# Windowed attention with a mixture of experts: another order for all engines, from a table

## The chip, the cores and the metric

The kernel runs on one core of one Trainium2 chip. The core has five engines with a queue of instructions each: PE (TensorE, matmuls, with its weight loads shown apart as PEld), DVE (VectorE), ACT (ScalarE), POOL (GpSimd) and SP (SyncE, which here only issues transfers). An engine runs its own instructions in the order in which they were written, and waits on semaphores for results of others and, in some cases, for its own. The metric is device time in microseconds (us), the median of several runs.

## What is computed

Two stages, with 8 batches, 8 heads, 576 positions, 64 columns a head. The first is attention with a window of 128 positions and a linear bias by distance; its output x of 576 x 512 a batch goes into the second, a mixture of four experts, of which each position uses its best two. Each expert is a causal attention with one head of 64 columns and an output projection to 512 columns.

```python
mask = (rel >= 0) & (rel < window)
scores = np.where(mask, scores + bias[None], -1000000000.0)
...
for e in range(E):
    q = x @ wq[e]; k = x @ wk[e]; v = x @ wv[e]
    scores = np.where(causal, -1000000000.0, scale * (q @ k.transpose(0, 2, 1)))
    ...
    ye = a @ v @ wo[e]
    for kk in range(K):
        mask = topk[:, :, kk] == e
        out += mask[..., None] * w[:, :, kk:kk + 1] * ye
```

## The kernel before

Work is cut by pairs of heads (four a batch, `g` counts all 32) in the first stage, and by batches `b` and pairs of experts `pr` in the second. A pair of heads is done in these steps: `attn_s` makes the scores of two blocks of 128 queries in one PSUM bank, `wrap` (L459) moves the far half of a window's columns over the near half with a masked copy on DVE (`copy_predicated`, two blocks of 128 columns at once), and `blocks` (L466) runs for each block a DVE instruction that adds the bias, scales and finds the row's minimum `nm` (CUSTOM_DVE_ANT_0 in the profile, ISA in the listings of the order; the read of its minimum, of shape 128x1, is a row of its own), and then an exponential on ACT. `normalise` (L472) sums and inverts on DVE and scales the rows (`scl`). `attn_t` transposes on PE; `split` (L561) writes the result apart on DVE. `attn_pv` (L597) multiplies with V, adds partial sums and writes x as two numbers, a rounded high part and the rest, into a tile named `wx`; the last 64 columns go through a small tile `xq` and then through `tail_out` (L644): a copy that rounds (CAST in the profile), and a subtraction. The second stage has projections with the same split into high and low parts (`QHm`, `KKm`, `AHm`, `ALm`), a gate per position, scores with minima `mnm`, normalising factors `mr` (L818), transposes (L837) and the output projection `moe_wo` (L895). Tiles named `w` are general work buffers of several pools, `ps` are the eight PSUM banks.

None of this is issued as it is written. The calls go to a recorder (`_Rec`), and some have an alternative: `evac` (a copy out of PSUM) and the copies of `tail_out` may go to ACT or DVE, `rnd` and `scl` to POOL or ACT, `ssub` to DVE or POOL. `plan` (L201) unpacks a table of numbers, `ORDER` (from L38 on), in which each number is a step back or forth in the list of recorded operations, times two, plus which of the alternatives to take; a negative place is a filler matmul, issued at the start. `place` (L160) then gives each tile a buffer of its pool in that order: a buffer is free again after the last operation on its old tile. The loop at L1190 issues the result, so nearly every row of the profile has line L1191. The order of each engine's queue, SP's transfers among them, thus follows from the table alone:

```python
    for lo, hi in zip(z[:n], z[n:]):
        d = lo + 256 * hi
        at += (d >> 1) ^ -(d & 1)
        ...
        i = nodes[at // 2]
        out.append(alt.get(i, [ops[i]])[at % 2])
```

Of the kernel before, what the change touches and what calls it, by code (L numbers as in the profile page):

```python
# [19 lines left out]
B, H, S, D = 8, 8, 576, 64  # L20
DM = H * D
E = 4
P = 128
# [27 lines left out]
    "W%a(atbaL<bLmqfAZ&%3z5M7=4nvLgXh1&{r;bFokbswGSIt(bK2%Mape~zLU-ryA%0<$-vCUNp*j4h+W73JD+c((Y=zB_Q26v~5IB&n;AbLe90|Ss&<Fg"
    "_IHVWhSKig$RjL2*#uK6?<*5|YpRqa{$Qmw_%Ff8B<~BIvk4#)i7OVv@Pa-_S9o^GgswC>y;YqPQ+pZ?t6vd?|u}rnAa;_(>)HhbbhR#Z}b7EI$k<;$12M"
    "b2aatJUBFpxl^>GZwr2YV|K_xK<@n8)j5aZ>zC<!#Z26pz&z(gw}LBaO{nl}e#n9j<iK!37<kZP1xt)YPk{5kk~C#a?M+v(Ws1|A7>$$u6d3MJv?P2Z{Zj"
    "Ihc<QPu$+f>17VtX+POrtgLHPp}L{b&g6*9?|g)@-(>H=Op61!>P>Hd>0QU@wCnpvJGs(V&{Wui-8F7s(jbHrqSy)3vVHTo5IjD2p>XVDF>iAgzvp67WEN"
    "FE@b`EzMuYhKB{R}x!YY6KWg6icUjF9S>=SdU;dR$vz0oMKFV5#lpKrDKl({w<pUucvcvo@*G9TrSw07WEtE>?!tF)#lpD-Iw=Z0E-v!XQqgVtgxUF?mfk"
    "tuSr+fGtqAeK2&Zcv^LKmaVqEH)z2$I(2%4vr2_y)GzA<`7_&h;&;&DA~>>UImBm66WZhgiJyzY-F;GM#BE`Jvy(rGu4SZ$LzL3M<$pXrcbjovwLq`g(_R"
    "Al2W3^v&iV(n=ia`9hq)6H6yieXVD$bNawsCcSXLf`>^wA;ZNW9YZAOt^aj7i{kRNQ%b@~FX5l(CZl<b>(A*|JagmfJuK7NF;aU_~pW}~igJlapwhHqQr="
    "m)J@ajyNmAtfkYFU8ge&090@$#S1#3ObLjDs6wLR>$2#|VGZ;RXnYSR{o5%q5K9%=83Zf^OyZAr7d}_ld**^wS%E@ju`8b__I@(<2+OQ$`-haDWjyeBfzl"
    "Qf2hq8N7b{eYK~)8fZUv<iz~MtbJkK#uUdCxwCmZ;b6|GiUB$mPoMf~1W@-ve6zmt)i^{G;>GYoRJgJ32#{?Rl}fRGkpe67NuPO9ls;J(uFzJzgrs(JKt0"
    "mR%Im7vyTD%QCM?RQT+^BgD&p)duI&Ey68GfREj{<~ke9#p(cdEPcSO`3HBM#ExYjn6*I$FGc-VqcC@TRUlw1Nx_Q5(!PdlvbesDj+r6>IdInyaNEL{*zw"  # L60
    "@&s4bCP_K5o6@^e%W#DW^56b2hE|$zAOCcW=J|B%3~jk&Dq-Izo4le8Zct%8PME|<P7U>8m_zXOJ9FS=M!O<8_O;w93nAnjkdsoe1HF>Sp|uGhL9$9jX6^"
    "i8{lXk3_n33?4!eBedU0k!2CVrg?oL2tMyREi9aX0HaEh>{r91l`xh%~PVeQom$a5^Dzx028lSJNQKf%`(Y=@m;!cfq#ipjv|0Ryciq=(~%HJb~6UK$!1G"
# [1216 lines left out]
```

## Time and profile before

| | |
|---|---|
| median of 3 runs | 500.97 us (500.94 to 501.03) |
| the profiled execution | 501.47 us |
| its span in the trace | 499.4 us, so 2.1 us lie around it |
| mean granted clock of PE | 0.998 |
| busy PE, PEld | 482.0 us, 411.5 us |
| busy DVE, ACT, POOL | 428.3 us, 365.1 us, 221.1 us |

A row of the profile names the line, the engine, the operation and its tiles as output<-input. Busy time of PE has modelled ends. An engine's share of the chain that ended last is the time that lay on that one path through all engines, so it is smaller than its busy share. The waits list, for a pair of waiting and awaited engine, the time in total, how often and the longest. Two rows of one engine may overlap in time: the next instruction can start while the one before it is still finishing.

### The profile page before, as it was taken

The numbers are of one execution on the slowest core, as the hardware profiler recorded it, in microseconds if no ns is written. First come the engines' busy times: TensorE is split into PE (matmuls) and PEld (weight loads), VectorE is DVE, ScalarE is ACT, GpSimd is POOL, SyncE is SP. The second block draws the span as 40 slices with busy tenths as digits, with TensorE's granted clock in tenths as the row PEclk, the third lists the DMA queues.
The fourth block names the chain that finished last, engine by engine and source line by source line (L and its number), as shares of the span: only waits on it lengthen the run. The fifth ranks groups of instructions, "written<-read, shape, count | busy, mean of one in ns | idle before, by whom it ended". The sixth has DMA issues, their size and how long they took to land.

```text
span 499.4 us, 17525 instructions
## 1 busy us (share of the span) xinstructions
PE 482.0 (97%) x6380; PEld 411.5 (82%) x6380; DVE 428.3 (86%) x1936; ACT 365.1 (73%) x1375; POOL 221.1 (44%) x456
## 2 busy tenths in 40 slices
PE   7999999999999999999999999999999999999996
PEld 5788888897788788798898987988778798799875
DVE  6999999989997999679988899798998979965842
ACT  5757878978878479596887869688786776853862
POOL 4724957072826205434461525707073523534250
PEclk9999999999999999999999999999999999999999
DMA  8879142107233035060442323620234031200033
GB/s 211 255 189 240 44 122 58 30 22 171 77 118 81 3 95 159 16 164 3 122 132 78 81 62 100 168 59 8 72 125 125 3 79 28 85 3 1 4 106 106
DMA packets 29862, 44.99 MB, mean 90 GB/s; under 512 B 9424, under 2 KB 15824, under 8 KB 29776
## 3 DMA queue, kind: packets, MB, share of 16 engines
q1 hardware_dynamic: 29040, 43.42, 31.8%
q8 instruction: 50, 0.82, 0.7%
q10 hardware_dynamic: 736, 0.46, 0.3%
q14 instruction: 36, 0.29, 0.2%
HBM read 34.42 MB, written 9.44 MB: 88 GB/s over the span
## 4 chain that ended last, share of the span: by engine, by line
PE 45%; DVE 35%; POOL 6%; ACT 5%; issue 4%; DMA 3%; SPq 1%; ACTq 0%; DVEq 0%; POOLq 0%
PE ps L1191 45%; DVE w L1191 21%; DVE ps L1191 6%; POOL w L1191 5%; ACT w L1191 4%; DMA w<-in_hd 2%; DVE mr L1191 1%; SPq L1191 1%; DVE ALm L1191 1%; DMA w<-in_wall 1%; DVE r L1191 1%; DVE wx L1191 1%; DVE KKm L1191 1%; DVE MPL L1191 1%; DVE nm L1191 0%
## 5 line engine op out<-in xcount | busy, mean ns | idle before, releaser
L1191 ACT COPY w<-ps 128x256 f32<-128x256 f32 (+2 forms) x217 | 87.7, 441 | 36.7 <-PE ps L1191 25.8
L1191 PE MATMUL ps<-wx,WH 128*128 128x288 f32 (+2 forms) x512 | 112.1, 303 | 1.8 <-DVE nm L1191 1.5
L1191 ACT ACTIVATE w<-w,nm 128x128 f32<-128x128 f32 x252 | 99.0, 396 | 17.1 <-DVE nm L1191 15.9
L1191 POOL TENSOR_SCALAR w<-w,r 128x128 f32<-128x128 f32 x176 | 66.1, 387 | 100.5 <-DVE mr L1191 29.7
L1191 POOL TENSOR_SCALAR w<-w,mr,w 128x512 f32<-128x512 f32 (+3 forms) x128 | 80.0, 634 | 45.0 <-DVE ps L1191 13.5
L1191 PEld LDWEIGHTS ps<-wx,WH 128*128 128x128 f32 x512 | 83.1, 189 | 5.2 <-DVE nm L1191 3.0
L1191 ACT ACTIVATE w<-w,mnm 128x512 f32<-128x512 f32 (+3 forms) x128 | 71.1, 557 | 17.2 <-DVE mnm L1191 16.5
L1191 DVE CUSTOM_DVE_ANT_0 w<-ps,tbt 128x128 f32<-128x128 f32 x288 | 72.9, 285 | 5.8 <-PE ps L1191 2.8
L1191 DVE TENSOR_TENSOR w<-ps,tmt 128x768 f32<-128x768 f32 (+3 forms) x96 | 72.3, 772 | 1.8 <-PE ps L1191 1.2
L1191 PE MATMUL ps<-wx,WL 128*128 128x288 f32 (+2 forms) x256 | 71.9, 297 | 0.0
L1191 PE MATMUL ps<-idt,w 64*128 64x64 f32 (+1 forms) x1152 | 62.1, 231 | 6.3 <-POOL w L1191 2.3
L1191 PE MATMUL ps<-w 64*64 64x192 f32 (+3 forms) x1256 | 62.9, 305 | 1.4 <-DVE nm L1191 0.7
L1191 PE MATMUL ps<-WH,wx 128*128 128x260 f32 x288 | 63.8, 288 | 0.2
L1191 PEld LDWEIGHTS ps<-idt,w 64*128 64x128 f32 (+1 forms) x1152 | 48.9, 139 | 18.3 <-POOL w L1191 6.0
L1191 PE MATMUL ps<-w,vt 64*64 64x192 f32 (+4 forms) x1344 | 59.2, 284 | 1.3 <-DVE nm L1191 0.7
L1191 PEld LDWEIGHTS ps<-w,vt 64*64 64x64 f32 (+1 forms) x1344 | 49.5, 133 | 8.4 <-issue 1.6
L1191 PEld LDWEIGHTS ps<-w 64*64 64x64 f32 (+1 forms) x1256 | 47.2, 134 | 10.8 <-DVE nm L1191 2.4
L1191 DVE COPY_PREDICATED ps<-mkt,ps 128x256 f32<-128x256 int32 (+2 forms) x160 | 50.6, 330 | 0.9
L1191 DVE CUSTOM_DVE_ANT_0 w<-ps,mtt 128x256 f32<-128x256 f32 (+2 forms) x96 | 50.2, 553 | 1.2 <-PE ps L1191 0.4
L1191 PEld LDWEIGHTS ps<-WH,wx 128*128 128x128 f32 x288 | 48.0, 189 | 2.0 <-DVE nm L1191 0.3
L1191 DVE COPY w<-ps 128x256 f32<-128x256 f32 (+3 forms) x93 | 42.5, 477 | 7.9 <-PE ps L1191 7.6
L1191 PE MATMUL ps<-w,w 128*64 128x64 f32 (+4 forms) x576 | 48.3, 319 | 0.3 <-DVE w L1191 0.2
(110 smaller groups left out, 961.6 us busy)
## 6 DMA issues: line engine op xcount, KB each, us to landing
w<-in_hd SPq DMA_DIRECT2D x56, 288.0 KB, 4.2
vt<-in_vd SPq DMA_DIRECT2D x28, 320.0 KB, 4.0
out<-w SPq DMA_DIRECT2D x31, 256.0 KB, 3.0
w<-in_hd SPq DMA_DIRECT2D x14, 128.0 KB, 3.9
w<-in_hd SPq DMA_DIRECT2D x56, 32.0 KB, 3.4
w<-in_wall SPq DMA_DIRECT2D x4, 386.0 KB, 5.5
out<-w SPq DMA_DIRECT2D x8, 128.0 KB, 2.4
vt<-in_vd SPq DMA_DIRECT2D x4, 192.0 KB, 4.6
```

What stands on the lines that cost most here:

```text
L1191: getattr(getattr(tc.nc, e), m)(*a, **k)
```

## The change

The table `ORDER` is replaced by another one, two lines shorter; nothing else is edited. The line that issues is L1189 instead of L1191. Operations, tiles and transfers are the same, and which buffer and which of its alternative engines an operation gets follows from the new table. The new table was made with a model in which VectorE and GpSimd wait for their own last result.

```diff
 ORDER = (
-    "c-p;re_Ui)b!WYIPrZBT_onO3)N`uVst5|PP?!M&89G7)1%+&pfd~m~U_!az!e_vMf&qnT$bf>vPNQ_}j`Ro$hTcFzo9<co1Pmy>(_~=-3LnA14j33|2NG"
...
+    "c-p;KeOO#sdB69bckVgKy_*?3v(C6PEBMS*Xc<c?bfFFvTIT7{9onHn1q&8jMnfAOVI35@ObZH?C_IHND7cB6)I>p{5*sSG@RU@dpu{B=Y_N$2g{NSHCKf"
...
 )
```

Of the table the diff can show no more than that it is another. What stands in the queues: DVE has 1,935 rows before and 1,902 now, ACT 838 and 880, POOL 459 and 454 instructions, PE 4,792 matmuls in both. DVE's instructions that wait for the result of the instruction straight ahead of them on DVE are 215 before and 109 now. POOL's are 50 and 45.

The first place is on DVE, in the scores of a pair of heads (the trace of before has it at 93.7 to 95.5 us). `ps` are PSUM banks with scores, `w` the tile of the probabilities, `nm` the minima; DVE_49 after "waits" is a wait for DVE's own earlier result, PE_49, Pool_49 and Activation_49 for the other engines. Before:

```order
L1191 COPY_PREDICATED ps_71<-mkt,ps_71 128x2x128 [waits PE_49]
L1191 ISA w_87,nm_183<-ps_71,tbt 128x128 [waits DVE_49]
L1191 ISA nm_183 128x1
L1191 ISA w_87,nm_183<-ps_71,tbt 128x128
L1191 ISA nm_183 128x1
L1191 COPY_PREDICATED ps_69<-mkt,ps_69 128x2x128 [waits PE_49]
L1191 ISA w_87,nm_183<-ps_69,tbt 128x128 [waits DVE_49]
L1191 ISA nm_183 128x1
L1191 ISA w_87,nm_183<-ps_69,tbt 128x128
```

Now:

```order
L1189 COPY_PREDICATED ps_73<-mkt,ps_73 128x2x128 [waits DVE_49,PE_49]
L1189 TENSOR_TENSOR ALm<-ps_74,AHm 128x512 [waits Activation_49]
L1189 ISA w_84,nm_183<-ps_73,tbt 128x128 [waits DVE_49,Pool_49]
L1189 ISA nm_183 128x1
L1189 ISA w_84,nm_183<-ps_73,tbt 128x128
L1189 ISA nm_183 128x1
L1189 COPY_PREDICATED ps_70<-mkt,ps_70 128x2x128 [waits PE_49]
L1189 ISA w_84,nm_183<-ps_70,tbt 128x128 [waits DVE_49]
L1189 ISA nm_183 128x1
L1189 COPY_PREDICATED ps_72<-mkt,ps_71 128x64 [waits PE_49]
L1189 ISA w_84,nm_183<-ps_70,tbt 128x128
```

Before, each pair of minima stands right behind the masked copy that it reads. Now the first masked copy has the subtraction that makes `ALm` behind it, and a third masked copy stands between the two minima of `ps_70`, the first of which still follows its own copy.

The second place is on DVE in `attn_pv` and `tail_out` (111 us in the trace of before): `xq` is the small tile, `wx` the tile of x. Before:

```order
L1191 TENSOR_TENSOR w_101<-w_101,ps_70 128x448 [waits PE_49]
L1191 TENSOR_TENSOR ps_75<-xq_184,ps_70 128x64 [waits Activation_49]
L1191 CAST wx_80<-ps_75 128x64 [waits DVE_49]
L1191 TENSOR_TENSOR wx_80<-ps_75,wx_80 128x2x64 [waits DVE_49]
L1191 COPY xq_198<-ps_71 128x64 [waits PE_49]
L1191 TENSOR_TENSOR ps_71<-xq_198,ps_76 128x64 [waits DVE_49]
L1191 TENSOR_TENSOR w_104<-w_104,ps_76 128x448 [waits Activation_49]
```

Now:

```order
L1189 TENSOR_TENSOR w_101<-w_101,ps_76 128x448 [waits PE_49]
L1189 TENSOR_TENSOR w_92<-ps_74,tmt 128x2x2x64
L1189 TENSOR_TENSOR ps_69<-xq_184,ps_76 128x64 [waits Activation_49]
L1189 TENSOR_TENSOR KKm<-ps_71,KKm 128x288
L1189 TENSOR_TENSOR wx_79<-ps_69,wx_79 128x2x64 [waits Activation_49]
L1189 COPY xq_198<-ps_70 128x64 [waits PE_49]
L1189 TENSOR_TENSOR ps_70<-xq_198,ps_75 128x64 [waits DVE_49]
```

and on ACT, now, at the same work:

```order
L1189 CAST KKm<-ps_71 128x288 [waits PE_49]
L1189 COPY xq_184<-ps_69 128x64 [waits PE_49]
L1189 CAST wx_79<-ps_69 128x64 [waits DVE_49]
L1189 ACTIVATE ex<-ex 128x5x4 [waits Pool_49]
L1189 COPY w_104<-ps_72 128x512 [waits PE_49]
L1189 CAST wx_81<-ps_70 128x64 [waits DVE_49,PE_49]
```

The rounding copy into `wx_80` stood on DVE between two instructions that need one another's results; it is on ACT now (`wx_79`), behind the copy of `xq`, and DVE has the subtraction for `KKm` between the sum and the subtraction that reads it.

## Rows read from the trace of the kernel before

**Rows 1.** The page: span, busy time by engine, chain that ended last.

```profile
span 499.4 us, 17525 instructions
...
PE 482.0 (97%) x6380; PEld 411.5 (82%) x6380; DVE 428.3 (86%) x1936; ACT 365.1 (73%) x1375; POOL 221.1 (44%) x456
...
PE 45%; DVE 35%; POOL 6%; ACT 5%; issue 4%; DMA 3%; SPq 1%; ACTq 0%; DVEq 0%; POOLq 0%
```

**Rows 2.** Busy time in three windows; the first line names the columns.

```profile
core 0: us, PE busy (x) PEld busy (x) DVE busy (x) ACT busy (x) POOL busy (x), PEclk, DMA share, GB/s
50.00:75.00 25.00, 24.71 (x382) 22.24 (x381) 24.64 (x113) 20.31 (x84) 17.73 (x39) 1.00 0.31 82
75.00:100.00 25.00, 24.46 (x335) 21.08 (x328) 23.99 (x126) 22.77 (x92) 10.55 (x21) 1.00 0.18 44
200.00:225.00 25.00, 24.55 (x313) 21.47 (x312) 17.90 (x87) 17.78 (x68) 11.03 (x21) 1.00 0.35 90
```

**Rows 3.** Waits of PE's weight loads: total us, times, longest us.

```profile
PEld ps L1191 <- DVE nm L1191: 8.6, 20, 1.1
...
PEld ps L1191 <- POOL w L1191: 6.2, 16, 0.8
...
PEld ps L1191 <- DVE w L1191: 4.9, 20, 0.4
...
PEld ps L1191 <- ACT w L1191: 4.5, 13, 1.2
...
PEld ps L1191 <- DVE mnm L1191: 3.0, 12, 0.4
```

**Rows 4.** DVE's timeline in the scores: start us, duration us, then the instruction.

```profile
93.78 0.42 DVE L1191 COPY_PREDICATED ps<-mkt,ps 128x256 f32<-128x256 int32 x1
94.24 0.29 DVE L1191 CUSTOM_DVE_ANT_0 w<-ps,tbt 128x128 f32<-128x128 f32 x1
...
94.45 0.29 DVE L1191 CUSTOM_DVE_ANT_0 w<-ps,tbt 128x128 f32<-128x128 f32 x1
...
96.83 0.42 DVE L1191 COPY_PREDICATED ps<-mkt,ps 128x256 f32<-128x256 int32 x1
97.16 0.16 DVE L1191 RECIPROCAL mr<-mr 128x1 f32<-128x1 f32 x1
97.23 0.27 DVE L1191 CUSTOM_DVE_ANT_0 w<-ps,tbt 128x128 f32<-128x128 f32 x1
```

**Rows 5.** DVE's timeline in `tail_out`.

```profile
111.48 0.22 DVE L1191 TENSOR_TENSOR ps<-xq,ps 128x64 f32<-128x64 f32 x1
111.74 0.22 DVE L1191 CAST wx<-ps 128x64 fp32r<-128x64 f32 x1
```

**Rows 6.** Copies out of PSUM by form: busy us, mean ns, then idle before.

```profile
L1191 ACT COPY w<-ps 128x512 f32<-128x512 f32 x95 | 54.0, 588 | 13.5 <-PE ps L1191 12.0 <-ACT AHTm L1191 0.6
...
L1191 ACT COPY w<-ps 128x256 f32<-128x256 f32 x66 | 23.2, 374 | 15.1 <-PE ps L1191 8.9 <-DVE lg L1191 5.6
...
L1191 DVE COPY w<-ps 128x512 f32<-128x512 f32 x31 | 20.9, 683 | 2.5 <-PE ps L1191 2.4
...
L1191 DVE COPY w<-ps 128x256 f32<-128x256 f32 x38 | 15.2, 416 | 4.0 <-PE ps L1191 3.9
...
L1191 ACT CAST wx<-ps 128x64 fp32r<-128x64 f32 x18 | 3.6, 208 | 2.1 <-DVE ps L1191 1.6 <-DVE mr L1191 0.4
...
L1191 DVE CAST wx<-ps 128x64 fp32r<-128x64 f32 x14 | 3.0, 218 | 0.2
```

**Rows 7.** Scalings and subtractions with a choice of engine, by form.

```profile
L1191 POOL TENSOR_SCALAR w<-w,r 128x128 f32<-128x128 f32 x176 | 66.1, 387 | 100.5 <-DVE mr L1191 29.7 <-DVE r L1191 19.7 <-DVE ps L1191 15.1
...
L1191 ACT ACTIVATE w<-w,r 128x128 f32<-128x128 f32 x112 | 39.9, 395 | 7.0 <-DVE r L1191 5.6 <-DVE wx L1191 1.1
...
L1191 POOL TENSOR_TENSOR wx<-w,wx 128x512 fp32r<-128x512 f32 x16 | 20.6, 1290 | 2.4 <-ACT wx L1191 1.7
...
L1191 DVE TENSOR_TENSOR wx<-w,wx 128x512 fp32r<-128x512 f32 x12 | 9.0, 749 | 1.7 <-POOL wx L1191 1.3 <-ACT wx L1191 0.5
```

More of the change, by code (lines that the diff above doesn't have):

```diff
@@ L111 @@
[L111 to L113 removed]
+    "c-p;KeOO#sdB69bckVgKy_*?3v(C6PEBMS*Xc<c?bfFFvTIT7{9onHn1q&8jMnfAOVI35@ObZH?C_IHND7cB6)I>p{5*sSG@RU@dpu{B=Y_N$2g{NSHCKf"
+    "6vY18-Id*=f-Yd`+z<zw#Lk8|GhzQ6bP{@x>q!mqqZIPsVeKYrOmGCYuFQ>%z-v8K{;h(b;Yo><!;<0MQmKgl4wblhq4x~Nh`ed(9xr+Q%|MU6nTiZGR#Z"
@@ new lines @@
+    "7iPxD*~#vIGGwEmPQ9aSsJs_AHUGCP}W}wETDQ)B1~=}&#Lq+yHpktsz@cXQCc6ORm?4aWJCUU#^8l_?ziudJWAZ&%sn)ub$`b*yz8`8vE}BG_JdXMusb-"
+    "_LvrcPz*^=+Q*-n*tX%E31QzE??nQ6G{A6)p0ono+`TqQ}Ebzd4q>QgW$6oi`u@mcWhYz0rG9~OWcR>__Q?}BcE`VH^%wa7NJGh{}*LNcb#r-hQI1SJXD@"
+    "%}@?-z19r}`|)!^OPGw!CwtMR=M;m~9H0ak(c!JI+!UovE;8Qk%nE&~$#}qJ^-D@_XKeIcEO^yc0qmfHeLfEn-&HM;FW!aB&3Y7=Q{z&=o4{^;Sb2^*IYX"
+    "h1AJXoq1V#R<OIki7)M@tD(HCAYo>h@M!b3;N$_Afl2<`F?Myi+*PzQVqx=nFdQllK$hRvGwhnZUo(6;pjecd6JL7ZyleHW`qQW_)#vX9#Y0n$KjVM?qvh"
@@ new lines @@
+    "=ohWOD1XFBlLQu{|A*l7v*=m;a!#uT;zA%K4MDn7EeR8cbSFAliQ6xvevp%9<|^8I)tIL_YwsSo!3=DR+e>8F+9YSxbzRSI60O6}loQQOS7F0-58e(pX0q"
+    "*AJy5g{3`{l<28O?Hbh`?}AcHxM)BBJ6FS>$Y`wo{yw5=LjKor=K=QoB2JGH$DL&5^)6V#ACJCQ=R9QW?a?9S87rr&Ff@smNQOv4P6V0y1r%g%vS(Z!b@)"
+    "-4-buoVe-H#{}HQ!X|<%3%#1fwltLK}dZ!itH9@2#2z9mfZh%xL`j{%zqOj`#a{v!J+v*zBsnEHZxkBB@+9t&^WMNijv8p!OpK^Qd!j+jt!ft=(yEo6lbv"
+    "TXBECd~maBX(9X>53Gtv*n^1);J~ruKTo^6=96hhYmupyp-|X(MdS`|D4+gBQ*YncL5%V^-RGm^(zRRTSuZ|8Ub6of@Cm+s8Mvl<1eg6meA`Lgq_T0hV9_"
@@ new lines @@
+    "Hem~6jW_XxkG`}5=g&-6=fZ{)!Of55ryl$KXIEFVa<lReKxrb)JJ-qT;=<QfM}H64!M@|MFJAe?r!3h4wSc|mgj&j)x`w{$Gj*E5Y&ENdq+1Gsdc4pB{X_"
+    "le+$w<4>tW(v7=);+cH_=gv@KXx)!-<8ph3O%EMbhWE||h^v)2p#BtY1`-ZQmM$I5(5_sXW)<fWd`e&%H5iY<D6<oubuP*&7;al2z~f2VE@SS5SYQ`xo;z"
+    "Quq<^<+hOmOb(K*2OhyFI&ix``L@8<HKqtQ!b7i2z1vBaL;QzJdZI0SyD3+=mz$apFT8BSJi`ivCAu)_-_rqBjFR|KV_TUr4Vvm0|P*#_6UavCPz6`l>Vx"
+    "82FfuX0vPsz4y&rR0CQWcn92++%}OUIk#>Azy0@?#7E+hb^n0vu$-Aie1YRrkstBmOjO<JW>5@=7=dePieDd9-VBWnta<M141H&_E#j8uJv(-Habwu%XT+"
@@ L114 @@
+    "BSf2M#*ESfiJny_Bi%^7@8adaSV2-psM90Q#Ms_~Nc4se5}mFTmsni&>VPz=CI2cCA-SY*AfsR=dj3iAjkiPwiDImhYFkJGHNDzqj-=y@$|M$oN9+L+t%M"
+    "p1HbJ~3w!tMOq!UR#<?71dYoeE6uIE8W?6KfdDPIq0n-^lNO-i(BiOoVjgs4j|DY>mCiI^FYfmq{sNckPvV@Xg*(k`y{LHJrBDNBqJh&Gy}cuAFz@k~OJM"
+    ";@(*jGiOr*2E^sAqG1v0b;d6-w_d$H*C0jL5O$vqR!=Dz&M`aI`PU}p(f3Pc2Lb?llXIFTw<S$9P!vI-;o|sMUz^0;s5jaFN-3z!T"
 )
```

130 lines of the change are left out of this document (56 added, 74 removed).

## The prediction

> **What bounds the kernel now.** I read the page first: the busy shares and the chain that ended last [rows 1]. PE is busy for 482.0 of 499.4 us (97%), DVE for 428.3 (86%), ACT for 365.1 (73%), POOL for 221.1 (44%). By shares alone PE is the bound, and only 499.4 - 482.0 = 17.4 us would be left to win. The chain says more: 45% of it is PE, 35% DVE, 6% POOL, 5% ACT. PE's ends are modelled, so a PE that is called busy may be waiting inside a modelled duration; the chain then passes through DVE.
>
> Second, the busy time by stages [rows 2]. From 50 to 75 us DVE works 24.64 us of 25.00 and from 75 to 100 us 23.99, level with PE (24.71 and 24.46). From 200 to 225 us DVE has 17.90 and PE still 24.55. So there are stages in which DVE feeds PE with nothing in hand, and stages in which its speed can't matter. ACT's worst stretch is 22.77 of 25.00, from 75 to 100 us.
>
> Third, what PE's weight loads wait for [rows 3]: DVE's row minima nm for 8.6 us in 20 waits, DVE's w for 4.9 in 20, DVE's mnm for 3.0 in 12: 16.5 us in 52 waits. POOL's w costs 6.2 and ACT's w 4.5. DVE is the engine waited for most.
>
> Fourth, single instructions of DVE [rows 4, 5]. Here one sees the price of a wait for an engine's own last result. The accumulated minimum that starts at 94.24 us runs 0.29 us, to 94.53, yet the next one, which needs nothing of it, starts at 94.45: an overlap of 0.08 us. The masked copy that starts at 93.78 and runs 0.42 ends at 94.20, and the minimum that reads its result starts at 94.24: 0.04 us after the end. At 111.48 a sum of 64 columns runs 0.22 us, and the rounding that reads it starts at 111.74: again 0.04 later. So a wait for the result straight ahead costs about 0.04 + 0.08 = 0.12 us; over all such pairs of the trace I worked out 0.114. With something independent between producer and reader most of this is gone: the masked copy at 96.83 and the minimum that reads it at 97.23 have a reciprocal between them; start to start is 0.40 us, in which the reciprocal is done too, against 0.46 with nothing between.
>
> **The change, part by part.** Operations, tiles and transfers stay; the table that sets the order changes, and with it the engine that takes an operation where there is a choice.
>
> *a. DVE's waits for its own last result.* Counted in the two orders, DVE's instructions that wait for the one straight ahead fall from 215 to 109, 106 fewer. At 0.114 us: 106 x 0.114 = 12.1 us of DVE's time [rows 4, 5]. POOL's fall from 50 to 45; its gaps in the trace are alike with and without such a wait, so I put that at nothing, and POOL at 44% covers it [rows 1].
>
> *b. Operations that leave DVE.* One fewer costs its mean less the overlap of 0.08 [rows 4, 6, 7]. Copies of 64 columns: 17 leave, x (0.218 - 0.08) = 2.3 us. Of 256 columns: 6 x (0.416 - 0.08) = 2.0. Of 512 columns: 9 x (0.683 - 0.08) = 5.4. Subtractions of 512 columns: 2 x (0.749 - 0.08) = 1.3. One subtraction for a weight of 772 columns, by columns 772/512 x 0.749 - 0.08 = 1.0. A few more leave or come, about nil. Sum 12.0 us. With a: 24 us, or 24/428.3 = 5.6% of DVE's work.
>
> *c. What ACT and POOL take on.* ACT: 17 x 0.208 + 6 x 0.374 + 9 x 0.588 = 11.1 us of copies, 11 scalings that leave POOL x 0.395 = 4.3, less three roundings of 512 columns that go to POOL, each taken as a copy of 512, 1.8: +13.6 us, 3.7% of ACT's 365.1 [rows 1, 6, 7]. POOL: 11 x 0.387 = 4.3 us less and 2 x 1.290 = 2.6 more, with the roundings and the weight's subtraction about +2 (an estimate), 1% of 221.1 [rows 1, 7].
>
> *d. PE's own order.* Its rows go from 3,769 to 3,749 with the same 4,792 matmuls. A matmul with its share of the busy time is 482.0/6380 = 0.076 us, and a merged row may stand for two: 20 x 2 x 0.076 = 3.0 us either way, value taken nil, since nothing is added or left out [rows 1]. The transfers are the same, in another order on SP; DMA is 3% of the chain, so a shift of 1% of the span, 5 us, would be the whole of what they could give or take if it all went one way; I take nil.
>
> *Sum.* DVE's saving counts where DVE is on the path. Upper value: the chain's DVE share, 35% of 499.4 = 174.8 us, shrinks by 5.6%: 9.8 us [rows 1]. Lower value: only PE's waits for DVE are shortened, 16.5 us, of which I take a fifth (3.3) to a half (8.2), since 5.6% less work lets DVE be earlier by more than a wait's mean of 16.5/52 = 0.32 us once three separated waits stand ahead of it [rows 3]. I take 8, between the half and the chain's value. Against it ACT's share of the chain grows: 5% of 499.4 = 25 us x 3.7% = 0.9, say 1. What is late next is ACT (its copies out of PSUM) and POOL's scalings. Net -7: 501.47 - 7 = 494.5 in the profiled execution, which took 0.5 us more than the median of the runs, 500.97: so **494.0**. Its own range: 9.8 + 3.0 = 13 us of gain, 488, to 3.3 less 1 of gain, 498.5.
>
> **A rule that speaks against it.** The trace shows 0.12 us between a DVE instruction with such a wait and one without [rows 4, 5]. The Trainium skill, "VectorE: DVE Perf Modes", section "The DRAIN you can't avoid", says that the next operation doesn't start until the pipe is empty and that a semaphore "costs nothing extra here": eight copies took the same time with one after each as with one after the last. The section also says that a next op that is not held starts earlier, and the trace shows this one here. By the first rule part a would be nil.
>
> **Rivals.**
>
> *1. Waits for own results cost nothing on the path.* The pairs that wait may be late for another reason (the pipe has to empty whichever instruction follows), so that separating them only moves idle time. Then b and c are left: 12.0/428.3 = 2.8% of 174.8 = 4.9 us, less 1 for ACT: 497.6 profiled, **497**. For it: in the pair at 96.83 to 97.23 the gain is only the reciprocal's slot. Against it: the overlap of 0.08 us behind 94.24 [rows 4]. The page named above is the rule for this. Chance 0.12.
>
> *2. PE sets the time.* At 97% busy, with DVE's waits at 16.5 us in all, earlier data would only wait for PE [rows 1, 3]. The gain is below 1 us and d decides: **500 to 502**. Against it: 35% of the chain on DVE. Chance 0.10.
>
> *3. ACT becomes late: slower.* Copies that leave DVE queue on ACT behind exponentials, PSUM banks come free later, and PE waits for a bank with everything behind it. The place is 75 to 100 us and stages like it: ACT has 2.23 us in hand there [rows 2]. Spread evenly, 13.6 us are 0.7 for each 25, and it fits; it decides as soon as a stage gets over three times its share. If so in many stages, the path gets two thirds of the 13.6, 9 us, while DVE gives back only the part of a, 12.1/428.3 x 174.8 = 4.9: +4, **505**; with all 13.6, 510. For it: 47 operations come to ACT. Against it: PE waits for ACT's w for only 4.5 us in 13 waits now, and ACT is 5% of the chain [rows 1, 3]. Chance 0.16.
>
> *4. The change doesn't do what it says.* The order of the changed kernel shows 109 of 215 left, so it does; no chance of its own.
>
> **How the numbers follow.** Forecast 0.62, rival 1 0.12, rival 2 0.10, rival 3 0.16. Runs of this kernel can tell some 0.2%, 1 us, from no change. Faster is forecast and rival 1: 0.74; the same is rival 2: 0.10; slower is rival 3: 0.16. The range begins at 488, the forecast's own end, and goes to 502.5, which takes in rivals 1 and 2 and the near edge of rival 3, so that about 0.2 is left out, most of it above.
>
> **What would show it.** Right: DVE busy near 408 us (428.3 - 12.0 - 106 x 0.08 = 407.8; the rest of a was idle time), ACT near 378, POOL near 223; PE idle below 17.4 us; DVE below 35% of the chain; PE's loads waiting for nm, w and mnm of DVE for under 10 us together; masked copy and minimum with another instruction between them. Wrong in a: such pairs as rare as counted, yet DVE's idle larger by what was saved. Wrong in c: PE's waits for ACT's w well over 4.5 us, ACT's share of the chain near 10%. Wrong in d: PE busy off by several us with the same waits.

## The result, and the profile after

The changed kernel takes 478.02 us (median, 476.78 to 478.22) against 500.96 us before in the same session: a ratio of 0.954, 95% interval 0.952 to 0.955. It is 23 us faster, where 7 were forecast, and the time lies below the range of 488.0 to 502.5. Of a_back, one of the experiments below, one run of four lies in a slower state (509.46 us at a granted clock of 0.851, the others at 0.994 or 0.995) and is left out of its number.

The page of the changed kernel: span, busy time by engine, and the chain that ended last, to be set beside [rows 1].

```profile
span 476.4 us, 17537 instructions
...
PE 468.2 (98%) x6380; PEld 409.5 (86%) x6380; DVE 410.3 (86%) x1900; ACT 371.0 (78%) x1416; POOL 218.2 (46%) x451
...
PE 80%; DVE 8%; DMA 4%; ACT 3%; SPq 2%; POOL 2%; issue 1%; DVEq 0%
```

In the traces DVE has 1,936 instructions before and 1,900 now, 36 fewer, where the rows counted in the order were 33 fewer. DVE is busy 410.3 us instead of 428.3 (407.8 was worked out), ACT 371.0 instead of 365.1, POOL 218.2 instead of 221.1. The surprise is PE: the same 6,380 instructions are now busy for 468.2 us instead of 482.0. Of the 23.0 us of span, 13.8 come out of PE's busy time and 9.2 out of its idle time. This pair of traces doesn't tell how much of the 13.8 us was waiting inside modelled ends and how much is PE's own new order. The run a_both below keeps PE's order of the changed kernel and is busy for 476.3 us, so 8.1 us come and go there with the waits. DVE's part of the chain has gone from 35% to 8%.

The same three windows as in [rows 2]:

```profile
core 0: us, PE busy (x) PEld busy (x) DVE busy (x) ACT busy (x) POOL busy (x), PEclk, DMA share, GB/s
50.00:75.00 25.00, 24.57 (x398) 21.64 (x397) 24.31 (x115) 20.91 (x87) 19.86 (x42) 1.00 0.37 95
75.00:100.00 25.00, 25.00 (x328) 22.94 (x327) 23.27 (x132) 24.16 (x99) 11.97 (x24) 1.00 0.07 20
200.00:225.00 25.00, 25.00 (x335) 22.53 (x332) 21.60 (x95) 21.04 (x82) 10.23 (x23) 1.00 0.30 80
```

PE is at 25.00 of 25.00 from 75 to 100 us and from 200 to 225 us. DVE is at 23 to 24 us in the two early windows as before, but the work goes by faster. The gain comes evenly: at each twentieth of PE's instructions the changed kernel is further ahead, by 3.6 us after the fourth, 12.8 after the tenth, 18.3 after the fifteenth and 23.0 at the last.

What PE's weight loads wait for (total us, times, longest us), as in [rows 3]:

```profile
PEld ps L1189 <- ACT w L1189: 4.3, 15, 0.7
...
PEld ps L1189 <- POOL w L1189: 3.4, 12, 0.9
...
PEld ps L1189 <- DVE mnm L1189: 2.1, 9, 0.4
...
PEld ps L1189 <- DVE w L1189: 1.4, 6, 0.4
...
PEld ps L1189 <- DVE nm L1189: 0.7, 4, 0.2
```

The minima nm have gone from 8.6 us in 20 waits to 0.7 in 4, DVE's w from 4.9 to 1.4. All rows of PE and PEld in the two views of waits whose awaited engine is DVE add up to 29.9 us in 91 waits before and 9.4 us in 37 after; with those for ACT, POOL and transfers it is 48.9 us before and 21.8 after (the rows called issue, 22.9 and 21.5 us, are left out). That fall of 27.1 us goes with the gain of 23.0; it needn't be equal to it, since a row of PE and one of PEld can count the same time.

DVE's timeline at the place that [rows 4] show of before (start, duration, instruction):

```profile
89.30 0.42 DVE L1189 COPY_PREDICATED ps<-mkt,ps 128x256 f32<-128x256 int32 x1
89.63 0.68 DVE L1189 TENSOR_TENSOR ALm<-ps,AHm 128x512 fp32r<-128x512 f32 x1
90.23 0.28 DVE L1189 CUSTOM_DVE_ANT_0 w<-ps,tbt 128x128 f32<-128x128 f32 x1
...
90.65 0.42 DVE L1189 COPY_PREDICATED ps<-mkt,ps 128x256 f32<-128x256 int32 x1
91.10 0.29 DVE L1189 CUSTOM_DVE_ANT_0 w<-ps,tbt 128x128 f32<-128x128 f32 x1
```

The masked copy at 89.30 has the subtraction for `ALm` behind it, which starts 0.09 us before the copy's end, and the minimum that reads it starts at 90.23, 0.08 us before the subtraction's end. The second copy, at 90.65, ends at 91.07, and its reader starts at 91.10: the old price, where nothing stands between. In the whole trace 99 of the 109 waits that are left have such a gap (median 0.034 us), as 200 of 215 had before.

### The profile page after: what moved, and what is told of

It reads as the page before. It is cut to its first block, busy times and chain, and to the rows that moved or that the text cites. A ratio compares the mean times of both kernels' runs of the same rounds, so it can differ in the third digit from the quotient of the medians.

```text
span 476.4 us, 17537 instructions
## 1 busy us (share of the span) xinstructions
PE 468.2 (98%) x6380; PEld 409.5 (86%) x6380; DVE 410.3 (86%) x1900; ACT 371.0 (78%) x1416; POOL 218.2 (46%) x451
## 4 chain that ended last, share of the span: by engine, by line
PE 80%; DVE 8%; DMA 4%; ACT 3%; SPq 2%; POOL 2%; issue 1%; DVEq 0%
PE ps L1189 80%; DVE w L1189 5%; ACT w L1189 2%; SPq L1189 2%; POOL w L1189 2%; DMA w<-in_hd 2%; DMA w<-in_rd 1%; DVE ps L1189 1%; DMA w<-in_wall 1%; DVE KKm L1189 0%; DVE r L1189 0%; DVE WL L1189 0%; DVE ALm L1189 0%; DVE mr L1189 0%; ACT QJm L1189 0%
## 5 line engine op out<-in xcount | busy, mean ns | idle before, releaser
L1189 ACT COPY w<-ps 128x512 f32<-128x512 f32 (+3 forms) x230 | 92.9, 449 | 31.1 <-PE ps L1189 20.1
L1189 PE MATMUL ps<-wx,WH 128*128 128x288 f32 (+2 forms) x512 | 110.6, 300 | 0.0
L1189 ACT ACTIVATE w<-w,nm 128x128 f32<-128x128 f32 x252 | 98.8, 395 | 7.5 <-DVE nm L1189 7.3
L1189 POOL TENSOR_SCALAR w<-w,r 128x128 f32<-128x128 f32 x165 | 60.6, 380 | 88.5 <-ACT w L1189 30.5
L1189 POOL TENSOR_SCALAR w<-w,mr,w 128x256 f32<-128x256 f32 (+3 forms) x128 | 78.2, 621 | 43.0 <-DVE mr L1189 15.8
L1189 PEld LDWEIGHTS ps<-wx,WH 128*128 128x128 f32 x512 | 83.3, 189 | 1.5 <-DVE mnm L1189 0.2
L1189 ACT ACTIVATE w<-w,mnm 128x256 f32<-128x256 f32 (+3 forms) x128 | 70.9, 557 | 14.4 <-DVE mnm L1189 13.0
L1189 DVE CUSTOM_DVE_ANT_0 w<-ps,tbt 128x128 f32<-128x128 f32 x288 | 72.5, 283 | 2.9 <-PE ps L1189 2.1
L1189 DVE TENSOR_TENSOR w<-ps,tmt 128x768 f32<-128x768 f32 (+3 forms) x96 | 72.4, 771 | 2.0 <-PE ps L1189 0.9
L1189 PE MATMUL ps<-wx,WL 128*128 128x288 f32 (+2 forms) x256 | 72.0, 296 | 0.0
L1189 PE MATMUL ps<-WH,wx 128*128 128x260 f32 x288 | 62.9, 287 | 0.0
L1189 PE MATMUL ps<-idt,w 64*128 64x64 f32 (+1 forms) x1152 | 60.4, 231 | 1.3 <-POOL w L1189 1.0
L1189 PE MATMUL ps<-w 64*64 64x192 f32 (+3 forms) x1256 | 58.9, 306 | 0.5 <-DMA w<-in_hd 0.4
L1189 PEld LDWEIGHTS ps<-idt,w 64*128 64x128 f32 (+1 forms) x1152 | 48.1, 139 | 11.4 <-issue 3.7
L1189 PE MATMUL ps<-w,vt 64*64 64x192 f32 (+4 forms) x1344 | 56.6, 284 | 0.4 <-ACT w L1189 0.4
L1189 PEld LDWEIGHTS ps<-w,vt 64*64 64x64 f32 (+1 forms) x1344 | 49.7, 133 | 6.5 <-ACT w L1189 1.0
L1189 DVE COPY_PREDICATED ps<-mkt,ps 128x128 f32<-128x128 int32 (+2 forms) x160 | 50.0, 329 | 2.4 <-PE ps L1189 2.0
L1189 PEld LDWEIGHTS ps<-w 64*64 64x64 f32 (+1 forms) x1256 | 45.0, 134 | 7.8 <-DMA w<-in_hd 1.6
L1189 DVE CUSTOM_DVE_ANT_0 w<-ps,mtt 128x384 f32<-128x384 f32 (+2 forms) x96 | 49.8, 551 | 1.0 <-PE ps L1189 0.6
L1189 PEld LDWEIGHTS ps<-WH,wx 128*128 128x128 f32 x288 | 48.4, 190 | 0.7 <-DVE nm L1189 0.2
L1189 PE MATMUL ps<-w,w 128*64 128x64 f32 (+4 forms) x576 | 48.2, 319 | 0.0
L1189 ACT ACTIVATION_READ_ACCUMULATOR w<-w,nm 128x1 f32 x252 | 48.2, 191 | 0.0
```

What stands on the lines that cost most here:

```text
L1189: getattr(getattr(tc.nc, e), m)(*a, **k)
```

## The experiments

Times in this section are medians; the kernel before took 501.04 to 501.29 us beside them, the changed kernel 478.02 (476.78 to 478.22; it wasn't run again beside them, so a difference of some 1 us from it says little). "A wait" is a wait of DVE for the result of the instruction straight ahead of it. The theories: T1, DVE's own time sets the end, and what is saved or added there counts nearly one for one; T2, the new order gains mostly by what PE finds ready, and DVE's time counts only by its share of the chain. T3 to T6 came later, and are told where they first stand. One thing besides the named change differs where the list is re-ordered (MOVE): `place` gives out the buffers again in the new order, so in a_both 3,365 of PE's 4,792 matmuls use another buffer, in b_sep3 3,638; what that alone is worth no run shows. Where only engines are exchanged (FLIP), and in b_less and a_less, the buffers stay.

**Putting the waits back into the changed order.** a_back exchanges a reader with the instruction ahead of it, so that it stands behind its producer again; a_moves gives 32 copies back to DVE at the place in the list that they have now; a_both does the two. The edit of a_both:

```diff
+FLIP = {
+    1385, 2061, 2185, 2303, 2653, 2686, 2857, 3044, 3362, 3364, 3555, 3647, 4034, 4040, 4193, 4540,
...
+}
+MOVE = (
+    (38, 37), (50, 39), (53, 52), (87, 86), (147, 146), (179, 178), (293, 292), (297, 294),
...
+)
...
 def plan(ops, alt):
...
-        out.append(alt.get(i, [ops[i]])[at % 2])
+        out.append(alt.get(i, [ops[i]])[(at + (i in FLIP)) % 2])
...
+    for i, j in MOVE:
+        out.insert(j, out.pop(i))
     return out
```

> The changed kernel with 95 operations of DVE exchanged with the one behind them, so that a reader stands straight behind its producer again: 200 waits for the result straight ahead instead of 109, nothing else moves. T1: 91 x 0.114 = 10.4 us more, 488 us. T2: by DVE's 8% of the chain of the changed kernel 0.8 us more, 479 us.

Measured: 486.25 us. 91 waits cost 8.2 us, 0.090 us each at the end of the kernel, near the 0.114 that one costs DVE.

> The changed kernel with 32 copies (17 of 64 columns, 6 of 256, 9 of 512) given back from ACT to DVE at the same place in the list; 115 waits for the result straight ahead instead of 109. DVE 9.7 + 0.7 = 10.4 us more. At 0.7 for one: 7.3 us more, 485 us. From the difference of a_both and a_back: 5.2 us more, 483 us. If the moves are only a matter of ACT's queue: faster or the same, 476 to 478 us.

Measured: 482.9 us, 4.9 us more for 7.8 us more of DVE's busy time (418.1 us), where 10.4 had been priced.

> The changed kernel with its readers straight behind their producers (208 such waits instead of 109) and the same 32 copies back on DVE. T1: 99 x 0.114 = 11.3 and 9.7 for the copies: 21 us more, 499 us, nearly the time before. T2: 8% of 21 = 1.7 more, 480 us.

Measured: 491.7 us, 13.7 us more; the two parts alone add up to 8.2 + 4.9 = 13.1. So waits and copies together are worth 13.7 us in the changed order, and 501.1 - 491.7 = 9.4 us are left with DVE's load put back. The page of a_both:

```profile
span 490.0 us, 17529 instructions
...
PE 476.3 (97%) x6380; PEld 410.7 (84%) x6380; DVE 424.8 (87%) x1932; ACT 365.3 (75%) x1384; POOL 219.2 (45%) x451
...
PE 61%; DVE 27%; ACT 7%; issue 3%; POOL 2%; DVEq 0%; ACTq 0%; POOLq 0%
```

DVE is busy 424.8 us, near the 428.3 of before, and yet the span is 9.4 us shorter.

**Taking waits out of the order before.** b_sep2 moves an operation of DVE up between a producer and its reader, 90 times, by the list alone; b_sep3 does it 88 times, but only with operations whose inputs the trace shows to be ready, and before readers whose result isn't wanted at once. a_sep2 and a_sep3 do the same to the changed kernel. The edit of b_sep3:

```diff
+MOVE = (
+    (95, 92), (120, 119), (139, 122), (137, 135), (229, 228), (362, 361), (403, 402), (491, 490),
...
+)
...
 def plan(ops, alt):
...
+    for i, j in MOVE:
+        out.insert(j, out.pop(i))
     return out
```

An earlier choice of such moves, in which some took a reduction past the reader of the same small buffer (part of the factors is then computed from other values, with the same work), came first, alone and with the 32 copies given to ACT:

> The kernel before with 89 operations of DVE moved up by a few places in the list, each between a DVE instruction and the next one that reads its result; engines of all operations as before. DVE's waits for the result straight ahead fall from 215 to 111, nothing else moves. Theory T1 (DVE's own time sets the end, nearly one for one): 104 waits x 0.114 us = 11.9 us less, 489 us. Theory T2 (the new order gains mostly by what PE finds ready, and a wait of DVE is worth only DVE's 35% of the chain): 0.35 x 11.9 = 4.2 us less, 497 us.

Measured: 501.28 us, no change; T1 and T2 both missed.

> The kernel before with 87 such moves on DVE and with 32 copies out of PSUM (17 of 64 columns, 6 of 256, 9 of 512) given from DVE to ACT at the same place in the list. Waits for the result straight ahead 215 to 107. T1: 108 x 0.114 = 12.3, and the copies 2.3 + 2.0 + 5.4 = 9.7: 22 us less, 479 us, the time of the changed kernel. T2: 0.35 x 22 = 7.7 less, 1 us more for ACT: 494 us.

Measured: 506.29 us, 1.0% slower than before. Both theories had it faster.

> The kernel before with 90 operations of DVE moved up by a few places in the list, each between a DVE instruction and the next one that reads its result; engines of all operations as before. 122 waits for the result straight ahead instead of 215. Theory T1 (DVE's own time sets the end wherever it is saved): 93 x 0.114 = 10.6 us less, 490.5 us. Theory T3 (what a wait gives back is lost again when its reader has to stand behind a foreign instruction, because PE waits for just these readers; only an order made as a whole gains): no change within 1 us, 501 us.

Measured: 502.47 us, 0.3% slower (ratio 1.003, 1.002 to 1.005). The time saved is lost on DVE itself: the waits of DVE in the trace of b_sep2,

```profile
DVE r L1209 <- ACT w L1209: 12.1, 15, 2.6
...
DVE w L1209 <- ACT w L1209: 2.6, 4, 1.0
DVE ALm L1209 <- ACT AHm L1209: 2.6, 3, 1.3
DVE QLm L1209 <- ACT QHm L1209: 2.5, 5, 0.7
...
DVE mr L1209 <- ACT MPL L1209: 1.7, 1, 1.7
```

beside those of the kernel before,

```profile
DVE r L1191 <- ACT w L1191: 8.2, 10, 1.7
...
DVE w L1191 <- ACT w L1191: 1.9, 3, 1.0
...
DVE QLm L1191 <- ACT QHm L1191: 1.7, 4, 0.7
...
DVE ALm L1191 <- ACT AHm L1191: 1.3, 1, 1.3
```

are longer: all rows of DVE waiting for ACT add up to 28.8 us instead of 18.0. 10.8 us more, and 10.6 was the saving as priced. Operations that were moved up stood at the head of DVE's queue and waited for ACT, with all of DVE behind them.

> The changed kernel with 44 operations of DVE moved up in the same way: 70 waits for the result straight ahead instead of 109. T1: 39 x 0.114 = 4.4 us less, 473.5 us. T3: no gain, 478 to 480 us.

Measured: 479.12 us, 1.1 us more, no gain as T3 had it.

> The kernel before with 88 other moves on DVE, chosen from its trace: the operation that is moved up had all its inputs ready before the reader started, and the first reader of the delayed result on another engine starts late enough to take the delay. 125 waits for the result straight ahead instead of 215. T1 (DVE's time is the end's time; b_sep2 lost its gain because moved operations waited for ACT at the head of DVE's queue): 90 x 0.114 = 10.3 us less, 491 us. T3 (any change of place in this order costs what it saves): 501 us.

Measured: 496.46 us, 4.8 us less (ratio 0.991, 0.989 to 0.992). Neither theory: with ready operations nearly half of the 10.3 us comes through.

> The changed kernel with 40 moves on DVE chosen from its own trace in the same way; 77 waits for the result straight ahead instead of 109. T1 at the 9.6/13.6 = 0.7 us that a_dve showed for each us of DVE: 32 x 0.114 x 0.7 = 2.6 us less, 475.5 us. T3: 478 to 479 us.

Measured: 478.00 us, no change. In the changed order the last waits that can be taken out this way are worth nothing.

**Less of DVE's work at the same places.** This takes DVE's time out without a change of place. The time of the shortened products, in b_less and in before:

```diff
-                split(diag_pair(w, 1, 3, D, D * h), ts[h][:, 2:, :], D, D * h)
+                n = D - 18 if g >= 8 else D
+                split(diag_pair(w, 1, 3, n, D * h), ts[h][:, 2:, :n], n, D * h)
```

> The kernel before with 48 of DVE's products that write the transposed probabilities apart shortened from 768 to 552 columns, from the ninth pair of heads on (18 of 64 columns are left out, which leaves old values there). No operation changes its place. By the copies of 512 and 256 columns a column costs (683 - 416)/256 = 1.04 ns: 48 x 216 x 1.04 ns = 10.8 us less on DVE. T1 (DVE's time pays one for one in this order, and the moves of b_sep3 cost the rest): 10.8 us less, 490 us. T5 (the order before gives back only about half, since its engines wait for one another at places that were timed without the waits): 5 us less, 496 us.

```profile
L1192 DVE TENSOR_TENSOR w<-ps,tmt 128x552 f32<-128x552 f32 x48 | 34.0, 724 | 1.5 <-PE ps L1192 0.9 <-ACT w L1192 0.3
```

```profile
L1191 DVE TENSOR_TENSOR w<-ps,tmt 128x768 f32<-128x768 f32 x56 | 52.3, 951 | 1.5 <-PE ps L1191 1.0 <-ACT w L1191 0.3
```

48 x (0.951 - 0.724) = 10.9 us of DVE were taken out, and DVE's busy time falls by 9.5 us to 418.8. Measured: 499.09 us, only 2.0 us less. This is the strongest result against the reasoning of the forecast. DVE's waits say where it went: for ACT 21.7 us instead of 18.0, for PE 25.9 instead of 23.7, for POOL 11.7 instead of 10.5, 7.1 us together. In this order the others are next in line right behind DVE, at least at these 48 places; all are one kind of instruction, between 86 and 434 us.

> The changed kernel with the same 48 products shortened, 10.8 us less on DVE. If PE has become the bound: under 3 us less, 475 to 478 us. If DVE still pays 0.7 for one, as in a_dve: 7.6 us less, 470.5 us.

Measured: 476.58 us, 1.4 us less; DVE's busy time falls by 8.9 us to 401.4.

**More work on DVE, and on PE.** 106 (104) copies that nobody reads, and 312 transposes done twice.

```diff
+        nc.alt["pad"] = ("vector", "tensor_copy", (m1.tile([P, D], F32, name="pad"), idt[:, :D]), {})
...
+    n, more = 0, []
+    for o in out:
+        n += o[0] == "vector"
+        if o[0] == "vector" and n > 100 and n % 13 == 0:
+            more.append(alt["pad"])
+        more.append(o)
+    out = more
     return out
```

> The kernel before with 106 extra copies of 128x64 on DVE, spread evenly, that nobody reads. Each about 0.134 us of DVE's time, 14.2 us; 15 of the own waits go with them (1.7 us): 12.5 us in all. T1: 12 us more, 513 us. T2 (only DVE's 35% of the chain counts): 4.4 us more, 505.5 us.

Measured: 514.02 us, 13.0 more. The price of 12.5 us was too low, as the copies' own row, one of them and the instruction on POOL beside it show:

```profile
L1199 DVE COPY pad<-idt 128x64 f32<-128x64 f32 x106 | 29.0, 274 | 0.0
...
119.85 0.79 DVE L1199 COPY pad<-idt 128x64 f32<-128x64 f32 x1
...
118.06 2.52 POOL L1199 TENSOR_TENSOR wx<-w,wx 128x512 fp32r<-128x512 f32 x2
```

A copy takes 0.274 us in the mean, not 0.214, and DVE's busy time rises by 17.2 us. Of the 106, 75 run for 0.215 us or less; the other 31 take up to 1.17 us, and 29 of these end about 0.05 us after an instruction of POOL ends, as the one at 119.85 does (120.64 us against 120.58). So a part of the added time looks like waiting for POOL inside DVE's busy time.

> The changed kernel with 104 of the same extra copies on DVE, 13.6 us. T1: 13 us more, 491 us. T2 (DVE is only 8% of the chain of the changed kernel): 1 us more, 479 us.

Measured: 487.6 us, 9.6 more; here DVE's busy time rises by 17.6 us, not 13.6.

Busy time and chain of b_dve, then of a_dve:

```profile
PE 488.6 (95%) x6380; PEld 413.1 (81%) x6380; DVE 445.5 (87%) x2042; ACT 365.7 (71%) x1375; POOL 220.2 (43%) x456
...
DVE 48%; PE 24%; POOL 10%; ACT 5%; issue 5%; SPq 3%; DMA 3%; ACTq 0%; DVEq 0%; POOLq 0%
```

```profile
PE 472.1 (97%) x6380; PEld 410.3 (84%) x6380; DVE 427.9 (88%) x2004; ACT 371.7 (77%) x1416; POOL 218.7 (45%) x451
...
PE 61%; DVE 24%; DMA 4%; SPq 3%; ACT 3%; issue 3%; POOL 1%; DVEq 0%; ACTq 0%
```

Against the rise of DVE's busy time, work added comes through to 0.76 in the order before (13.0 of 17.2 us) and to 0.55 in the changed one (9.6 of 17.6), though its chain had only 8% of DVE: with 104 more copies the same chain has 24%. Work taken out came through to 0.2 (b_less). A chain's share holds for neither direction.

```diff
+    n, more, k = 0, [], 0
+    while k < len(out):
+        o = out[k]
+        g = [o]
+        while len(g) + k < len(out) and o[1] == "transpose" and out[k + len(g)][1] == "transpose" and len(g) < 2:
+            g.append(out[k + len(g)])
+        more += g
+        if len(g) == 2:
+            n += 1
+            if n % 4 == 0:
+                more += g
+        k += len(g)
+    out = more
     return out
```

> The kernel before with 312 transposes on PE done twice, in pairs spread evenly over all transposes; 47.1 us / 1088 = 0.043 us each, 13.5 us of PE. T1 (DVE bounds the kernel before, PE's 97% holds waits): under 5 us more, 501 to 506 us. Rival T4 (PE bounds it, as its busy share says): 12 to 13.5 us more, 514 us.

Measured: 507.39 us, 6.2 more.

> The changed kernel with the same 312 transposes done twice, 13.5 us of PE. T1 (the bound has gone over to PE, 80% of the chain): 9 to 13 us more, 487 to 491 us. T4: 13.5 us more, 491 us, as with the kernel before.

Measured: 484.89 us, 6.9 more. Busy time and chain of b_pe, then of a_pe:

```profile
PE 489.4 (97%) x6692; PEld 421.2 (83%) x6692; DVE 429.4 (85%) x1936; ACT 365.3 (72%) x1375; POOL 219.7 (43%) x456
...
PE 50%; DVE 32%; POOL 5%; ACT 4%; issue 3%; DMA 3%; SPq 2%; ACTq 0%; DVEq 0%; POOLq 0%
```

```profile
PE 474.7 (98%) x6692; PEld 417.3 (87%) x6692; DVE 411.6 (85%) x1900; ACT 372.1 (77%) x1416; POOL 218.2 (45%) x451
...
PE 91%; DVE 4%; ACT 1%; DMA 1%; POOL 1%; SPq 1%; issue 1%; DVEq 0%
```

Both theories missed: the two orders answer alike. The price was too high, too. PE's weight loads are busy for 9.7 us more in b_pe and 7.8 in a_pe, not 13.5, so 312 transposes cost about 8 to 10 us and most of it arrives in either kernel (6.2 of 9.7 us and 6.9 of 7.8). The chain's 45% and 80% of PE have the same order but not the size. PE wasn't free in the kernel before, and it isn't the only bound after.

**Copies and waits together in the order before, and the choices alone.** b_moves gives the 32 copies to ACT in the order before, b_both3 does this together with 83 moves of the kind of b_sep3, and a_allflip gives all 298 operations whose engine differs back to the engine they had before, in the changed order. The edits are FLIP and MOVE as above with other numbers.

> The kernel before with the same 32 copies given from DVE to ACT; DVE 9.7 us less and 8 waits fewer (0.9). T1: 10.6 us less, 490 us. T6 (a copy that joins ACT's queue in an order not made for it holds back the exponentials behind it): slower than before, 502 to 506 us.

Measured: 504.89 us, 3.8 us slower, as the theory of ACT's queue had it. All rows of DVE waiting for ACT add up to 29.3 us instead of 18.0, which fits it; which copies held back what isn't shown.

> The kernel before with the 32 copies given from DVE to ACT (as in b_moves) and 83 moves on DVE chosen from the trace (as in b_sep3): 123 waits for the result straight ahead instead of 215, DVE's load within some us of the changed kernel's. If DVE's load makes the time: 92 x 0.114 + 9.7 = 20 us less, 481 us. If the parts add up as measured alone (-4.8 and +3.8): 500 us. If the order makes the time: 498 to 503 us.

Measured: 500.39 us; the parts alone, -4.8 and +3.8, give -1.0 and the ratio to before is 0.999 (0.998 to 1.000). The page:

```profile
span 498.8 us, 17525 instructions
...
PE 481.8 (97%) x6380; PEld 412.7 (83%) x6380; DVE 413.7 (83%) x1904; ACT 371.4 (74%) x1407; POOL 218.9 (44%) x456
...
PE 45%; DVE 35%; ACT 9%; POOL 5%; issue 4%; DMA 1%; ACTq 0%; DVEq 0%; SPq 0%; POOLq 0%
```

DVE is busy 413.7 us, 3.4 above the changed kernel's 410.3, and the span is 22.4 us longer than its 476.4. DVE's idle time tells the two orders apart. In the order before it is 71.1 us, in b_both3 85.1: of 14.6 us that DVE works less, 14.0 come back as idle time, in b_less 7.2 of 9.5 and in b_sep3, the part that gained, 1.8 of 6.7. In the changed order it is 65.2 us with the load put back (a_both) and 66.1 without: of 14.5 us that DVE works less, 0.9 come back. This holds for the load that the order was made with, not for less: a_less, with 8.9 us less work, has 73.4 us of idle time.

> The changed kernel's order with every one of the 298 operations that went to another engine given back to the engine it had before, at the same place in the list. DVE's instructions are 1936 again and 118 wait for the result straight ahead. If only DVE's net load counts: 36 more operations, 12 us, at 0.5 to 0.7 for one 6 to 8 us more, 484 to 486 us. If the single choices were timed with the order: 490 us or more.

Measured: 536.5 us, 58.5 us slower than the changed kernel and 35 slower than the one before. The page, and three of PE's waits:

```profile
span 535.2 us, 17534 instructions
...
PE 492.0 (92%) x6380; PEld 421.5 (79%) x6380; DVE 421.6 (79%) x1936; ACT 364.4 (68%) x1375; POOL 217.3 (41%) x456
...
PE 41%; DVE 29%; ACT 15%; POOL 7%; issue 4%; DMA 2%; SPq 1%; POOLq 0%; DVEq 0%; ACTq 0%
```

```profile
PEld ps L1212 <- POOL w L1212: 19.8, 21, 4.9
...
PEld ps L1212 <- ACT w L1212: 15.6, 21, 4.1
...
PE ps L1212 <- POOL w L1212: 15.4, 11, 4.8
```

One window of a_allflip, with the columns of the windows in the section on the result:

```profile
200.00:225.00 25.00, 20.22 (x243) 18.51 (x241) 13.35 (x50) 10.66 (x34) 9.37 (x17) 0.86 0.20 61
```

DVE's load is between the two kernels', its waits for the result straight ahead are 118, and all of that means little: PE waits for POOL's and ACT's w, with single waits up to 4.9 us, which fits operations that stand in the queue of an engine that gets to them late. Not all of the 58.5 us need be these waits: the mean granted clock of PE is 0.971 here against 0.996 in the changed kernel, with windows such as the one shown, where PE is busy for only 20.22 of 25 us and the granted clock, for a part of them at its lower level of 1.2 GHz, is 0.86 in the mean. The time not granted is (1 - 0.971) x 535.2 = 15.5 us here and 1.9 there, so up to some 13.6 us may be the clock's (an estimate). Whether the waits brought the clock down, no run tells.

The four corners, in us:

| | DVE's load as before | DVE's load as changed |
|---|---|---|
| order before | 501.1 | 500.4 (b_both3) |
| changed order | 491.7 (a_both) | 478.0 |

The order alone, with most of its choices of engine, gives 9.4 us, the load alone 0.7, both 23.1. The load of b_both3 was brought about with moves of its own, so it is near the changed kernel's in size, not in place. The span goes with the sum of PE's and PEld's waits for other engines, from all rows of those views. The sum and the span: 21.8 and 476.4 (changed), 38.0 and 490.0 (a_both), 40.7 and 494.5 (b_sep3), 47.1 and 498.8 (b_both3), 48.9 and 499.4 (before), 67.1 and 512.1 (b_dve), 100.9 and 535.2 (a_allflip). Above the changed kernel the span of these rises by 0.7 to 1.0 us for each us of these waits (least in b_sep2, with 57.3 and 500.8). The two kernels with more work on PE lie off this line, as they should (a_pe has 20.7 and 482.4). DVE's busy time, in the same order, doesn't sort them: 410.3, 424.8, 421.6, 413.7, 428.3, 445.5 and 421.6.

## Why the prediction was right or wrong

**What bounds the kernel.** The statement that "only 499.4 - 482.0 = 17.4 us would be left to win" by shares was wrong, though what follows it doubted it: 23.0 us were won, and PE's busy time fell by 13.8 us with the same instructions. It still shaped the lower end of 488. That DVE is the engine waited for most was right: 20.5 of the 27.1 us that PE waits less are waits for DVE.

**Parts a and b, DVE's time.** Right in the counts and on DVE: busy 410.3 us, 407.8 worked out. Waits for the result straight ahead have the price that was read: a_back pays 0.090 us each at the end. This speaks clearly against rival 1; an exchange also moves the other instruction back by one place, and no run has that part alone. The Trainium skill, "VectorE: DVE Perf Modes", section "The DRAIN you can't avoid", has it for its eight copies that the semaphore costs nothing extra; here, by a_back, 91 such waits cost 8.2 us, and the traces show 0.034 us of gap with the wait against about 0.08 us of overlap without.

Two of the readings behind this were wrong. The minimum at 97.23 us doesn't read the masked copy at 96.83: it starts before that copy ends (97.25), and what it reads was finished before; so this pair shows neither a gain by a reciprocal in between nor, under rival 1, the lack of one. The gaps of the 46 waits before that have one instruction in between show it instead: their median is an overlap of 0.083 us. POOL's gaps, too, aren't alike with and without a wait, as the last section shows; for 5 waits fewer that is 0.5 us of POOL's time.

**Part c, ACT and POOL.** ACT rose by 5.9 us of busy time, not 13.6, and POOL fell by 2.9 instead of rising by 2. The durations of ACT's instructions do add up to 13.6 us more (493.1 against 479.5); busy time counts the stretch in which two of them overlap only once, and the overlap that part b took off for each of DVE's was not taken off here. The idle that ACT had was enough here, since rival 3 didn't come: PE's loads wait for ACT's w for 4.3 us, as before 4.5. But what it feared can happen. In the order before, b_moves pays 3.8 us for the same 32 copies.

**The sum: the step that failed.** "DVE's saving counts where DVE is on the path", sized with the chain's 35% and with a fifth to a half of the 16.5 us of PE's waits in three rows. Two things are wrong with it. It is mis-sized: all rows of waits for DVE on PE and PEld hold 29.9 us, of which 20.5 went. And its mechanism is wrong: it treats the change as the old order with a shorter DVE. That was run, and gains next to nothing: 2.0 us for 10.9 us less work in place (b_less), 4.8 for waits taken out with care (b_sep3), 0.7 with the copies too (b_both3). In the old order what DVE saves comes back for the most part as its idle time (14.0 of 14.6 us in b_both3, 7.2 of 9.5 in b_less); in the changed one it doesn't (0.9 of 14.5, between a_both and the changed kernel). The gain is of order, choice of engine and load together, and the worth of the order was what the prediction had set at nil under d. That 24 us of DVE's time and 23 us of gain are so near is chance: with nearly that load put back, a_both loses only 13.7 us.

**Rivals and signs.** Rival 2 fell with PE's busy time. Of the signs, DVE's busy time, PE's idle time (8.2 us), the chain's share and the waits for nm, w and mnm (0.7 + 1.4 + 2.1 = 4.2 us, under 10) came as named; they would have come with 7 us of gain as well, so they didn't tell the size. ACT (378) and POOL (223) didn't come as named. The sign against d, PE busy off by several us with the same waits, can't be read off this pair, since the waits changed too. The nearest is b_sep3, with PE's old order, 40.7 us of waits and 479.6 us busy, beside a_both, with the new one, 38.0 and 476.3: 3.3 us of busy time for 2.7 us of waits.

**What stays open.** Which of the 298 choices and which moves make the 9.4 us of the order was not tried one by one; a_allflip shows only that they belong to the order. PE's own new order and the buffers that go with it were never changed alone, so a few us may be theirs. That a model with the waits in it places operations better is argued, not shown: no run here changes the model. And why most of the work added on DVE comes through while work taken out doesn't is shown by DVE's waits for ACT, PE and POOL in b_less only in sum, not place by place.

## What to carry to other kernels

When a whole order is made anew, don't price it as the old order with some costs removed: single parts put into the old order gave between 4.8 us of the 23 (b_sep3) and a loss of 3.8 (b_moves), and the engine choices of one order put into the other cost 58 (a part of it perhaps by the clock). After each such trial, see whether the time saved on an engine has come back as its idle time. Read what the bound engine waits for over all rows of its waits, its weight loads among them, and take that sum (48.9 us here, of which 21.8 were left) as the upper mark of what there is to win, rather than its idle time (17.4 us); this rests on one kernel. On DVE, put an independent instruction that is already ready between a result and its reader; one that has to wait itself can cost more than the 0.11 us that it saves (b_sep2). And don't price added work by its shortest form: the copies of b_dve took 0.274 us, not 0.214.

## What the runs showed of the hardware

A wait of DVE for the result of the instruction straight ahead costs about 0.114 us of DVE's time (0.034 us of gap against 0.08 us of overlap), and behind one other instruction nearly nothing: the median gap at that distance is an overlap of 0.083 us, in both traces. POOL pays for such a wait as well. In the trace of before:

```profile
57.62 0.24 POOL L1191 TENSOR_SCALAR QJm<-QHm 64x64 fp32r<-64x64 f32 x1
57.82 0.62 POOL L1191 TENSOR_SCALAR wx<-w 128x512 fp32r<-128x512 f32 x1
58.52 1.27 POOL L1191 TENSOR_TENSOR wx<-w,wx 128x512 fp32r<-128x512 f32 x1
```

The rounding at 57.82, which waits for nothing of POOL's, starts 0.04 us before the end ahead of it; the subtraction that reads its result starts 0.08 us after its end. All 43 such waits of POOL's tensor instructions before have a gap of 0.082 us or more (median 0.087 in the 27 shortest), where instructions that follow at once without such a wait overlap by 0.022: about 0.11 us a wait. A copy of 128x64 from SBUF to SBUF on DVE runs for about 0.19 us (median in b_dve and a_dve), but in 58 of the 60 cases in which it took over 0.215 us it ended about 0.05 us after an instruction of POOL. 312 transposes done twice, 0.043 us each by busy time, cost PE's weight loads only 0.025 to 0.031 us each.
